# Head of a fused attention and feed-forward kernel: the second slot's first Q and K by shifted weight columns, its first score row earlier, four V tiles moved forward

## The chip, the cores and the metric

The kernel runs as one program on one core of a Trainium2 chip. A core has five engines with a queue of instructions each: TensorE (PE in the profile; its weight loads are PEld) multiplies matrices into the eight banks of PSUM, VectorE (DVE), ScalarE (ACT) and GpSimd (POOL) work elementwise or reduce, and SyncE (SP) issues transfers. Each engine runs its own instructions in the order written and waits at semaphores for the others. The metric is the device time of one execution in microseconds (us), here as the median of several runs.

## The reference

A block with two halves over a sequence of 2048 tokens of 512 features (bfloat16), with 32 heads of 16:

```python
qkv = (layernorm(x) @ wqkv).reshape(B, S, 3, H, Dh) -> q, k, v
scores = einsum("bhqd,bhkd->bhqk", q, k) * (Dh ** -0.5)
p = softmax(scores, axis=-1)
h = x + einsum("bhqk,bhkd->bhqd", p, v).reshape(B, S, D) @ wo
h2 = h + (gelu(layernorm(h) @ w_gate) * (layernorm(h) @ w_up)) @ w_down
```

The scores are 32 x 2048 x 2048, so some 134 million of them pass through a maximum and an exponential; the matrix products beside them are small. The feed-forward half is 1792 wide.

## The kernel before

The 32 heads lie in 8 *slots* of 4 heads. A slot's Q and K are stored transposed, with 16 features of a head at the head of each of four 32-partition groups and room for the negated maximum behind them (`QT`, `KT`). A projection of 128 weight columns yields 8 heads at 16 partitions each: the even heads lie on partitions 0, 32, 64, 96 and are slot `2*ht`; the odd heads lie 16 partitions lower down and are slot `2*ht+1`. To bring those to the right partitions the kernel before copies the projection to `QKS`, moves it up by 16 partitions with a transfer to `QKS2`, and masks the result into `QT` or `KT` on POOL (`item_projT`, and for the first chunk `head_qks` and `head_shift`).

The queries come in 12 *groups* (four of 256 tokens, eight of 128). A group and a slot make a *unit*, 96 in all. Attention runs in two passes over each unit:

- Pass 1 finds the maximum of each query. One *row* is 128 queries of two heads against 512 keys (a *chunk*, `kc`): two matmuls into a pair of PSUM banks (L776) and one DVE reduction over 1024 columns (L779). There are 1024 rows. Unit 0 is the first group and slot 0, unit 1 the first group and slot 1. When a unit's last row is done, POOL joins the maxima, splits them into three bfloat16 parts, a transposing transfer (`STG`) turns them, and POOL adds them to `QT`. Rows 0 to 7 belong to units 0 and 1 and chunk 0; units 8 and 9 (the second group) may lend up to eight rows when the next row isn't ready.
- Pass 2 computes the scores transposed (L927), with the maximum already subtracted through the extra rows, and ACT takes the exponential of 512 columns at a time (L936). There are 2048 of these. They are multiplied by V (L958), and then come normalization, output projection, layernorm, and the feed-forward half of the group, all interleaved with later units.

Nothing of this order is fixed by hand beyond the head: a planner (`Plan`) walks through the program with estimated durations for each instruction and decides what each engine is given next. The estimates (`ivl`, `lat`) therefore shape the order of the whole program, but each engine then simply runs that order and waits where it must. POOL's work comes from a list of jobs with priorities (`jobs.add`, a smaller number first); ACT's statistics come from `act_jobs`; projections and V tiles are *items* that the planner slips in between rows.

The head of the kernel, which the change rewrites, is written out by hand: four tiles of x are normalized and transposed (`head_T`), Q of tokens 0 to 255 and K of tokens 0 to 511 are projected for slot 0 (`head_mm`, then `head_q` and two evacuations), Q of tokens 256 to 511 follows, the four PSUM results are copied once more into `QKS`, and two transfers on SP (L1425) with two masks on POOL (L1430) make slot 1's K and Q. Meanwhile DVE has taken the statistics of x tiles 4 and 5, and ACT takes those of tiles 6 to 15 (`late_stats`, L1466): a sum and a sum of squares per tile. `ln_chain` then finishes them on POOL and normalizes tile by tile (L545), PE transposes each tile (L552), ACT evacuates it to `xnT` (L554), and `item_projT` projects K of the next chunk. V tiles (`item_projV`, matmuls at L714, evacuated by ACT at L590) may start only while few ACT jobs are waiting (`len(act_jobs) <= AJ`).

Of the kernel before, what the change touches and what calls it, by code (L numbers as in the profile page):

```python
# [262 lines left out]
def bass_sequential_preLN__mha_block__geglu_ffn__prompt_kernel(nc, A_x, A_wqkv, A_wo, B_x, B_w_gate, B_w_up, B_w_down, out):  # L263
    with ExitStack() as es:
# [103 lines left out]
        def dve(fn, reads, writes, ivl, lat, extra=()):  # L368
            return P.op("dve", fn, reads, writes, ivl, lat, extra=extra)
# [146 lines left out]

        def ln_norm_act(t):
            act(lambda e: e.activation(out=xn_sb[:, t, :], in_=x_sb[:, t, :], func=ACT.Identity, bias=nmr1[:, t:t + 1], scale=rstd[:, t:t + 1]),
                [("x", t), ("rstd", t), ("nmr1", t)], [("xn", t)], 512, lat=0.79, ivl=0.69)

# [3 lines left out]

        DNORM = {}

        def ln_chain(ts, have_mv):
# [7 lines left out]
            else:  # L535
# [4 lines left out]
            ops += [o(lambda e: e.tensor_tensor(out=rstd[:, sl], in0=rstd[:, sl], in1=nhalf[:, sl], op=ALU.pow), k("rstd") + ["nhalf"], k("rstd"), 0.5 + 0.155 * len(ts), 0.44 + 0.155 * len(ts)),  # L540
                    o(lambda e: e.tensor_tensor(out=nmr1[:, sl], in0=htmp[:, sl], in1=rstd[:, sl], op=ALU.mult), k("rstd") + lk + nk * (not have_mv), nk)]
            for t in ts:
                if t in DNORM:
                    continue
                ops.append(o(lambda e, t=t: e.tensor_scalar(out=xn_sb[:, t, :], in0=x_sb[:, t, :], scalar1=rstd[:, t:t + 1], scalar2=nmr1[:, t:t + 1], op0=ALU.mult, op1=ALU.add),  # L545
                             [("x", t), ("rstd", t)] + nk, [("xn", t)], 0.74, 0.78))
            jobs.add(1, ops)

# [35 lines left out]
        p2_on = [False]  # L584

        def evac(o_ap, i_ap, reads, writes, n, extra=()):
            if p1_over[0] and P.eng["dve"].free <= P.eng["act"].free:
                return dve(lambda e: e.tensor_copy(out=o_ap, in_=i_ap), reads, writes, n / 960.0 + 0.063, n / 960.0 + 0.17, extra=extra)
            last_extra[0] = exps[0]
            return act(lambda e: e.activation(out=o_ap, in_=i_ap, func=ACT.Copy), reads, writes, n, extra=extra)  # L590
# [61 lines left out]
        def item_projT(it, which, ht, c):  # L652
            nm = "w" + which + ("0" if ht == 0 else "")
            tk = list(range(4 * c, 4 * c + 4))
            for d in range(4):
                yield 0.22, [nm] + [("xnT", t) for t in tk], "f"
                b = it.b
                if d == 0:
                    si, s2 = qk_n[0] % 4, qk_n[0] % 2
                    qk_n[0] += 1  # L660
                    qks_busy[("a", si)] = qks_busy[("b", s2)] = True
                for dc in (d,):
                    P.mm(lambda e, dc=dc: e.matmul(pbank[:, b, :], w_cols(which, dc, ht), xnT[:, dc, 512 * c:512 * c + 512], start=(dc == 0), stop=(dc == 3)),
                         reads=[nm] + [("xnT", t) for t in tk], writes=[("pb", b)], n=512, sig=(dc == 3))

# [57 lines left out]

        p1_on = [False]
        seq = []
        steps_of = lambda ui: [(kc, qh, gp) for kc in range(4) for qh in range(nq_of(units[ui][0])) for gp in range(2)]
# [676 lines left out]

        def head_mm(which, b, c0, c1):
            nm = "w" + which + "0"
            xk = [("xnT", t) for t in range(c0 // 128, c1 // 128)]
            for dc in range(4):
                if dc == 0:
                    fill(P.ready("pe", [nm] + xk), 7)
                P.mm(lambda e, dc=dc: e.matmul(pbank[:, b, 0:c1 - c0], w_cols(which, dc, 0), xnT[:, dc, c0:c1], start=(dc == 0), stop=(dc == 3)),  # L1410
                     reads=[nm] + xk, writes=[("pb", b)], n=c1 - c0, sig=(dc == 3))

        def head_q(b, c0, c1, eng):
            keys = [("qT", 0, t) for t in range(c0 // 128, c1 // 128)]
            if eng == "dve":
                return dve(lambda e: e.tensor_scalar(out=QT[:, 0, 0, c0:c1], in0=pbank[:, b, 0:c1 - c0], scalar1=qmask[:, 0:1], scalar2=None, op0=ALU.mult), [("pb", b), "qmask"], keys, 0.33, 0.43)
            else:
                act(lambda e: e.activation(out=QT[:, 0, 0, c0:c1], in_=pbank[:, b, 0:c1 - c0], func=ACT.Copy, scale=qmask[:, 0:1]), [("pb", b), "qmask"], keys, c1 - c0, lat=0.5, ivl=0.4)

        def head_qks(si, b, c0, c1, extra=()):  # L1420
            keys = [("QKSp", si, c0)] + ([("QKS", si)] if c1 == 512 else [])
            return act(lambda e: e.activation(out=QKS[:, si, c0:c1], in_=pbank[:, b, 0:c1 - c0], func=ACT.Copy), [("pb", b)], keys, c1 - c0, extra=extra)

        def head_shift(si, c0, o_ap, keys, s1, s2_):
            P.dma("sp", lambda e: e.dma_start(out=QKS2[0:112, si, :], in_=QKS[16:128, si, :]), ("qks", si), reads=[("QKS", si), ("QKSp", si, 0), ("QKSp", si, c0)], writes=[("QKS2", si)], lat=2.2)  # L1425

            def over(t):
                qks_busy[("a", si)] = qks_busy[("b", si)] = False
                qkv_check()
            jobs.add(1, [(lambda e: e.tensor_scalar(out=o_ap, in0=QKS2[:, si, :], scalar1=s1[:, 0:1], scalar2=s2_[:, 0:1], op0=ALU.mult, op1=ALU.add),  # L1430
                          [("QKS2", si), "qmask", "kmask", "kbias", "zero1"], keys, 0.74, 0.78, ())], then=over)

        for k_ in range(2):
            qks_busy[("a", k_)] = qks_busy[("b", k_)] = True
        qk_n[0] = 2
        qkv_left[0] = 16 + 16 + 16 - 2
        head_T(0)
        head_T(1)
        head_T(2)
        head_mm("q", 6, 0, 256)  # L1440
        t_q = head_q(6, 0, 256, "dve")
        ln_stats(5)
        head_T(3)
        head_mm("k", 4, 0, 384)
        act(lambda e: e.activation(out=KT[:, 0, 0:384], in_=pbank[:, 4, 0:384], func=ACT.Identity, bias=kbias[:, 0:1], scale=kmask[:, 0:1]), [("pb", 4), "kmask", "kbias"], [("kTh", 0)], 384, lat=0.65, ivl=0.55)
        head_mm("k", 5, 384, 512)
        t_k = dve(lambda e: e.tensor_scalar(out=KT[:, 0, 384:512], in0=pbank[:, 5, 0:128], scalar1=kmask[:, 0:1], scalar2=kbias[:, 0:1], op0=ALU.mult, op1=ALU.add), [("pb", 5), "kmask", "kbias", ("kTh", 0)], [("kT", 0, 0)], 0.2, 0.3)
# [9 lines left out]
        DST, AJ = {}, 2  # L1457

        def late_stats(ts):
            left = [2 * len(ts)]  # L1460
            for t in ts:
                for (func, dst, key) in ((ACT.Copy, hsum, "hs1"), (ACT.Square, hsq, "hq1")):
                    pi = 2 * (t - 6) + (func == ACT.Square)

                    def go(t=t, func=func, dst=dst, key=key, pi=pi):
                        act(lambda e: e.activation(out=PTM[:, pi, :], in_=x_sb[:, t, :], func=func, accum_out=dst[:, t:t + 1]), [("x", t)], [(key, t), ("PT", pi)], 512, ivl=0.62, lat=0.95)  # L1466
                        left[0] -= 1
                        if left[0] == 0:
                            ln_chain(ts, False)
                    act_job(go, [("x", t)], [("PT", pi)])  # L1470
        row_hooks = {}
        ln_chain([4, 5], True)
        late_stats([6, 7])
        for t, r in DNORM.items():
# [215 lines left out]
```

## Time and profile before

| | us |
|---|---|
| median of 3 runs | 1240.42 |
| lowest, highest | 1239.35, 1242.41 |
| the profiled execution: its time | 1239.89 |
| the profiled execution: its span | 1238.2 |
| DVE busy | 1191.8 |
| ACT busy | 1195.8 |
| PE busy | 1162.9 |
| POOL busy | 806.1 |
| first row's reduction on DVE starts | 11.93 |
| first exponential on ACT starts | 58.48 |
| last row's reduction on DVE ends | 1199.0 |

The times of the table's last three lines are counted from the start of the span. Most of the program is steady: DVE reduces one row after another, ACT takes one exponential after another, and PE feeds both. What differs from that is the first 60 us, in which rows run but exponentials can't yet, and the last 40 us, in which no rows are left. A busy time counts an instruction from its start to its end, and neighbours overlap a little, so a share near 100% can still hold small gaps.

### The profile page before, as it was taken

To read this page: it belongs to the slowest core of one execution; us is meant where nothing else is said; L and a number is where in the kernel's file an instruction comes from. 1 tells how busy PE (TensorE), PEld (TensorE's weight loads), DVE (VectorE), ACT (ScalarE), POOL (GpSimd) and SP (SyncE) were. 2 spreads that over 40 slices of the span, in tenths; PEclk is the share of its full clock that TensorE was granted. 3 is DMA by queue.
4 is the path that set the end of the run, shared out by engine and by line. 5 is a ranking of instruction groups with operands and counts; after the bars stand their busy time and mean duration, and the time that the engine had idled before them with its cause. 6 is when DMAs were issued, how large, how long until landed. Compare 5 with 4: busy or idle time off the path is not lost.

```text
span 1238.2 us, 39549 instructions
## 1 busy us (share of the span) xinstructions
PE 1162.9 (94%) x16813; PEld 609.8 (49%) x16944; DVE 1191.8 (96%) x1141; ACT 1195.8 (97%) x2515; POOL 806.1 (65%) x1637
## 2 busy tenths in 40 slices
PE   7999999999999999999999999999999999999998
PEld 3333333344333443334345665565666656656666
DVE  6999999999999999999999999999999999999982
ACT  6699999999999999999999999999999999999995
POOL 6757733788537884678727788277584948474854
PEclk8999999999999999999999999999999999999999
DMA  4011150000010000100001000000000010000000
GB/s 145 28 35 35 34 183 21 14 6 4 10 27 13 6 6 12 27 10 3 7 24 18 15 10 10 15 19 6 20 9 19 11 19 10 18 11 10 16 18 11
DMA packets 53137, 28.25 MB, mean 23 GB/s; under 512 B 38240, under 2 KB 51936, under 8 KB 52960
## 3 DMA queue, kind: packets, MB, share of 16 engines
q1 hardware_dynamic: 51904, 25.45, 7.9%
q8 instruction: 133, 2.18, 0.7%
q14 instruction: 44, 0.36, 0.1%
q10 hardware_dynamic: 1056, 0.26, 0.1%
HBM read 11.80 MB, written 2.10 MB: 11 GB/s over the span
## 4 chain that ended last, share of the span: by engine, by line
ACT 55%; DVE 18%; PE 17%; POOL 6%; DMA 2%; issue 2%; SPq 0%; POOLq 0%; DVEq 0%; ACTq 0%
ACT PTM L936 33%; DVE PM L779 17%; ACT PTG L936 9%; ACT PTE L936 5%; PE pbank L927 4%; PE pbank L776 3%; PE pbank L453 2%; PE pbank L1181 2%; ACT g_sb L590 2%; ACT th_sb L1162 2%; PE pbank L1209 2%; PE pbank L958 1%; ACT u_sb L590 1%; POOL LINV L992 1%; ACT OA L590 1%
## 5 line engine op out<-in xcount | busy, mean ns | idle before, releaser
L779 DVE TENSOR_REDUCE PM<-pbank 128x2 f32<-128x1024 f32 x1016 | 1163.8, 1214 | 13.1 <-PE pbank L776 5.3
L936 ACT ACTIVATE PTM<-pbank 128x512 bf16<-128x512 f32 x1388 | 729.1, 656 | 4.3 <-PE pbank L927 2.7
L927 PE MATMUL pbank<-QT,KT 32*128 32x128 bf16 (+1 forms) x6144 | 616.5, 235 | 25.2 <-ACT PTM L936 3.1
L776 PE MATMUL pbank<-KT,QT 32*128 32x512 bf16 x2048 | 400.5, 387 | 24.3 <-DVE PM L779 11.2
L927 PEld LDWEIGHTS pbank<-QT,KT 32*128 32x128 bf16 x6144 | 308.1, 92 | 220.5 <-issue 73.4
L936 ACT ACTIVATE PTG<-pbank 128x512 bf16<-128x512 f32 x420 | 228.2, 661 | 2.0 <-PE pbank L927 0.8
L776 PEld LDWEIGHTS pbank<-KT,QT 32*128 32x128 bf16 x2048 | 97.2, 91 | 181.1 <-DVE PM L779 81.0
L453 PE MATMUL pbank<-ones_bf 128*128 128x512 bf16 (+1 forms) x444 | 134.0, 372 | 9.3 <-issue 1.7
L958 PE MATMUL pbank<-PTM,VA 128*17 128x128 bf16 (+1 forms) x4164 | 133.4, 238 | 1.7 <-ACT PTG L936 0.3
L936 ACT ACTIVATE PTE<-pbank 128x512 bf16<-128x512 f32 x240 | 132.7, 673 | 0.1
L992 POOL TENSOR_TENSOR LINV<-OAT,negone 128x4 f32<-128x4 f32 (+1 forms) x94 | 115.0, 1234 | 19.8 <-ACT OAT L590 19.5
L958 PEld LDWEIGHTS pbank<-PTM,VA 128*17 128x17 bf16 x4164 | 77.2, 90 | 36.5 <-issue 16.5
L860 POOL TENSOR_TENSOR QT<-QT,STG 128x128 bf16<-128x128 bf16 (+1 forms) x95 | 48.3, 508 | 70.0 <-DMA STG<-ST 69.3
L832 POOL CAST ST<-NEGM 128x4 bf16<-128x4 f32 (+1 forms) x95 | 19.7, 208 | 85.5 <-DVE NEGM L840 83.1
L453 PEld LDWEIGHTS pbank<-ones_bf 128*128 128x128 bf16 x524 | 39.6, 98 | 69.9 <-ACT PTM L936 21.7
L815 POOL TENSOR_TENSOR MX<-PM,MX 128x8 f32<-128x8 f32 x94 | 19.0, 202 | 76.7 <-DVE PM L779 73.7
L1168 POOL TENSOR_TENSOR th_sb<-th_sb,g_sb 128x512 f32<-128x512 f32 (+1 forms) x56 | 67.3, 1201 | 1.4
L1164 POOL TENSOR_TENSOR th_sb<-th_sb,g_sb 128x512 f32<-128x512 f32 (+1 forms) x56 | 67.3, 1201 | 1.3
L1152 POOL TENSOR_TENSOR GUT<-th_sb,u_sb 128x512 bf16<-128x512 f32 (+1 forms) x56 | 67.1, 1201 | 1.3
L1181 PE MATMUL pbank<-hnT_l,wu_sb 128*128 128x128 bf16 (+1 forms) x616 | 66.9, 240 | 0.8
L1181 PE MATMUL pbank<-hnT_l,wg_sb 128*128 128x128 bf16 (+1 forms) x616 | 66.2, 242 | 1.2 <-issue 0.3
L1166 POOL TENSOR_TENSOR th_sb<-g_sb 128x512 f32<-128x512 f32 (+1 forms) x56 | 55.3, 988 | 15.3 <-ACT g_sb L590 15.1
(159 smaller groups left out, 1137.6 us busy)
## 6 DMA issues: line engine op xcount, KB each, us to landing
QKS<-QKS SPq DMA_DIRECT2D x32, 112.0 KB, 2.2
xres<-in_A_x_dram SPq DMA_DIRECT2D x16, 128.0 KB, 2.3
out_dram<-out_sb SPq DMA_DIRECT2D x15, 128.0 KB, 1.7
wg_sb<-in_B_w_gate_dram SPq DMA_DIRECT2D x4, 448.0 KB, 5.3
wu_sb<-in_B_w_up_dram SPq DMA_DIRECT2D x4, 448.0 KB, 8.1
x_sb<-in_A_x_dram SPq DMA_DIRECT2D x3, 512.0 KB, 6.6
STG<-ST SPq DMA_TRANSPOSE x96, 2.3
wd_sb<-in_B_w_down_dram SPq DMA_DIRECT2D x3, 512.0 KB, 4.9
```

The source lines that it names most:

```text
L453: P.mm(lambda e: e.matmul(pbank[:, b, 0:n], ones_bf[:, 0:128], ones_bf[:, 0:n], start=True, stop=True), reads=["ones_bf"], writes=[("pb", ...
L776: P.mm(lambda e, g=g, b=b0 + jj: e.matmul(pbank[:, b, :], QT[32 * g:32 * g + 32, c, slot, col:col + 128], KT[32 * g:32 * g + 32, slot, 512 ...
L779: dve(lambda e: e.tensor_reduce(out=pmv(par, kc)[:, qh, 2 * gp:2 * gp + 2], in_=pbank[:, b0:b0 + 2, :], axis=AX.X, op=ALU.max), [("pb", b0 ...
L927: P.mm(lambda e, kt=kt, i=i: e.matmul(pbank[:, b, w * i:w * i + w], KT[32 * g:32 * g + 32, slot, 128 * kt:128 * kt + 128], QT[32 * g:32 * ...
L936: act(lambda e: e.activation(out=PTt(pi), in_=pbank[:, b, :], func=ACT.Exp), [("pb", b)], [("PT", pi)], 512, lat=0.605, ivl=0.48, extra=dX)
L958: P.mm(lambda e, g=g, kt=kt, pi=pi, i=i: e.matmul(pbank[32 * g:32 * g + 17, b, 0:w], VA[:, kt, head(slot, g), :], PTt(pi)[:, w * i:w * i + ...
L992: inv = [((lambda e, a=a: e.tensor_tensor(out=LINV[:, par, a:a + hh], in0=oat[:, a:a + hh, 16], in1=negone[:, 0:hh], op=ALU.pow)), [("OAT" ...
L1152: jobs.add(3, [o(lambda e: e.tensor_tensor(out=o_ap, in0=shp(ts_), in1=shp(us), op=ALU.mult), [kt, ku], [("GUT", fc) for fc in fcs], 1.25, ...
L1164: o(lambda e: e.tensor_tensor(out=ts_, in0=ts_, in1=gs, op=ALU.mult), [kt, kg], [kt], 1.25)], then=second)
L1166: jobs.add(3, [o(lambda e: e.tensor_tensor(out=ts_, in0=gs, in1=gs, op=ALU.mult), [kg], [kt], 1.03, dE), o(lambda e: e.tensor_scalar(out=t ...
L1168: o(lambda e: e.tensor_tensor(out=ts_, in0=ts_, in1=gs, op=ALU.mult), [kt, kg], [kt], 1.25)], then=first)
L1181: P.mm(lambda e, dc=dc, fc=fc, i=i: e.matmul(pbank[:, it.b, w * i:w * i + w], wsb[:, dc, 128 * fc:128 * fc + 128], hT[:, dc, 0:w], start=( ...
```

## The change

Slot 1's first chunk of Q and K is no longer moved by transfers. The two small weight loads of the head bring 144 columns in place of 128, and the same projection is run a second time with the weight columns shifted by 16 (`w_cols(..., sh=16)`), so that the odd heads come out on the even heads' partitions. ACT evacuates the results straight to `KT` and `QT` with scale and bias. The four copies to `QKS`, the two transfers and the two POOL masks of the head go. The first row is issued behind K of slot 1 and ahead of Q of slot 1 and the second half of slot 0's Q. The statistics of tiles 6 and 7 are issued in the head, between its evacuations, and `ln_chain` splits into statistics at priority 0.5 and normalizations at priority 1. V tiles 0 to 3 no longer wait until few ACT jobs are queued (`VE = 4`).

```diff
-        load_w(0, "wq0", 4.0, 0, 128, "act")
-        load_w(1, "wk0", 4.3, 0, 128, "act")
+        load_w(0, "wq0", 4.0, 0, 144, "act")
+        load_w(1, "wk0", 4.3, 0, 144, "act")
...
-        load_w(1, "wk", 7.9, 128, D)
-        load_w(0, "wq", 8.7, 128, D)
+        load_w(1, "wk", 7.9, 144, D)
+        load_w(0, "wq", 8.7, 144, D)
...
-        DNORM = {}
+        DNORM, ANORM = {}, ()
...
-            jobs.add(1, ops)
+
+            def over(tt):
+                for i_, t in enumerate([t for t in ts if t in ANORM]):
+                    act_jobs.insert(i_, (lambda t=t: ln_norm_act(t, nk), [("x", t), ("rstd", t)] + nk, [("xn", t)]))
+                if norms:
+                    jobs.add(1, norms)
+            jobs.add(0.5, ops, then=over)
...
-        def w_cols(which, dc, ht):
-            base = (0 if which == "q" else D) + 128 * ht
+        def w_cols(which, dc, ht, sh=0):
+            base = (0 if which == "q" else D) + 128 * ht + sh
             return wqkv_sb[:, dc, base:base + 128]
...
+        LAG0, LAGX = 2000, lambda n: 60
+
         def evac(o_ap, i_ap, reads, writes, n, extra=()):
-            if p1_over[0] and P.eng["dve"].free <= P.eng["act"].free:
+            if (p1_over[0] and P.eng["dve"].free <= P.eng["act"].free) or (p1_i[0] >= LAG0 and not p1_over[0] and 2 * p1_i[0] - exps[0] > LAGX(p1_i[0])):
...
-            nm = "w" + which + ("0" if ht == 0 else "")
+            nm = ["w" + which + "0"] + ["w" + which] * (ht > 0)
...
+        ops67 = deque()
+        late_stats([6, 7], ops67)
...
+        def head_k(slot, b, c0, c1, key, reads=()):
+            act(lambda e: e.activation(out=KT[:, slot, c0:c1], in_=pbank[:, b, 0:c1 - c0], func=ACT.Identity, bias=kbias[:, 0:1], scale=kmask[:, 0:1]), [("pb", b), "kmask", "kbias"], [key], c1 - c0, lat=(c1 - c0) / 1200 + 0.33, ivl=(c1 - c0) / 1200 + 0.23)
...
         head_mm("k", 4, 0, 384)
-        act(lambda e: e.activation(out=KT[:, 0, 0:384], in_=pbank[:, 4, 0:384], func=ACT.Identity, bias=kbias[:, 0:1], scale=kmask[:, 0:1]), [("pb", 4), "kmask", "kbias"], [("kTh", 0)], 384, lat=0.65, ivl=0.55)
+        head_k(0, 4, 0, 384, ("kTh", 0))
+        ops67.popleft()()
         head_mm("k", 5, 384, 512)
...
-        head_mm("q", 7, 256, 512)
-        head_qks(0, 6, 0, 256, [t_q])
-        head_qks(1, 4, 0, 384)
-        tok = head_qks(1, 5, 384, 512, [t_k])
-        sp_when(P.at[tok], lambda: head_shift(1, 384, KT[:, 1, 0:512], [("kT", 1, 0)], kmask, kbias))
-        tok = head_qks(0, 7, 256, 512)
-        sp_when(P.at[tok], lambda: head_shift(0, 256, QT[:, 0, 1, :], [("qT", 1, t) for t in range(4)], qmask, zero1))
-        head_q(7, 256, 512, "act")
-
+        head_mm("k", 6, 0, 512, 16)
+        head_k(1, 6, 0, 512, ("kT", 1, 0))
+        ops67.popleft()()
+        fill(p1_ready(), 7)
+        p1_issue()
+        head_mm("q", 4, 0, 512, 16)
+        head_q(1, 4, 0, 512, "act")
+        head_mm("q", 5, 256, 512)
+        ops67.popleft()()
+        ops67.popleft()()
+        head_q(0, 5, 256, 512, "act")
         DST, AJ = {}, 2
+        VE = 4
...
-            add_item(*it, can=can_projT if it[0] is item_projT else lambda i_: len(act_jobs) <= AJ)
+            add_item(*it, can=can_projT if it[0] is item_projT else lambda i_: len(act_jobs) <= AJ or i_.args[0] < VE)
```

Line numbers of the changed file are about 10 higher than those of the file before: L776, L779, L927, L936, L590 and L714 there are L786, L789, L937, L946, L599 and L723.

More of the change, by code (lines that the diff above doesn't have):

```diff
@@ L1402, in head_T @@
             ln_T(4 + t % 2, t)
[L1404 to L1431, printed above, removed]
@@ L1453, in bass_sequential_preLN__mha_block__geglu_ffn__prompt_kernel, with late_stats @@
[L1453 to L1459 removed]
+        def late_stats(ts, now=None):
             left = [2 * len(ts)]
@@ L1469, in go, with head_mm @@
                             ln_chain(ts, False)
-                    act_job(go, [("x", t)], [("PT", pi)])
-        row_hooks = {}
+                    if now is None:
+                        act_job(go, [("x", t)], [("PT", pi)])
+                    else:
+                        now.append(go)
+        ops67 = deque()
+        late_stats([6, 7], ops67)
+        def head_mm(which, b, c0, c1, sh=0):
+            nm = "w" + which + "0"
+            xk = [("xnT", t) for t in range(c0 // 128, c1 // 128)]
+            for dc in range(4):
+                if dc == 0:
+                    fill(P.ready("pe", [nm] + xk), 7)
+                P.mm(lambda e, dc=dc: e.matmul(pbank[:, b, 0:c1 - c0], w_cols(which, dc, 0, sh), xnT[:, dc, c0:c1], start=(dc == 0), stop=(dc == 3)),
+                     reads=[nm] + xk, writes=[("pb", b)], n=c1 - c0, sig=(dc == 3))
```

47 lines of the change are left out of this document (26 added, 21 removed).

## The prediction

> **What bounds the kernel now.** I read the busy times first, then the two ends of the program engine by engine, then the waits of the head.
>
> ```profile
> PE 1162.9 (94%) x16813; PEld 609.8 (49%) x16944; DVE 1191.8 (96%) x1141; ACT 1195.8 (97%) x2515; POOL 806.1 (65%) x1637
> ```
>
> DVE and ACT are both nearly full. A stretch of 33 rows on DVE takes 37.41 us in the chain, 1.134 us a row; exponentials follow each other every 0.49 us (21 in 10.59 us, less the overlap). From 11.93 us (first row) to 1199.0 us (last) DVE has 1187 us for 1024 x 1.134 = 1161 us of rows, so it lost some 26 us, and the head is where they lie thickest. DVE's order of time from the head's last evacuation on:
>
> ```profile
> 11.03 0.41 DVE L1447 TENSOR_SCALAR KT<-pbank,kmask,kbias 128x128 bf16<-128x128 f32 x1
> 11.93 4.62 DVE L779 TENSOR_REDUCE PM<-pbank 128x2 f32<-128x1024 f32 x4 [0.49 <-PE pbank L776]
> 19.50 2.35 DVE L779 TENSOR_REDUCE PM<-pbank 128x2 f32<-128x1024 f32 x2 [2.96 <-PE pbank L776]
> 22.30 1.23 DVE L779 TENSOR_REDUCE PM<-pbank 128x2 f32<-128x1024 f32 x1 [0.45 <-PE pbank L776]
> 24.24 1.23 DVE L779 TENSOR_REDUCE PM<-pbank 128x2 f32<-128x1024 f32 x1 [0.71 <-PE pbank L776]
> 26.31 1.22 DVE L779 TENSOR_REDUCE stats<-pbank 128x2 f32<-128x1024 f32 x1 [0.85 <-PE pbank L776]
> ...
> 35.75 24.74 DVE L779 TENSOR_REDUCE PM<-pbank 128x2 f32<-128x1024 f32 x21
> ```
>
> Rows 0 to 15 take 35.75 - 11.93 = 23.82 us in place of 18.14: 5.68 us idle. What ended it, by the waits from 10 to 60 us:
>
> ```profile
> ACT xnT L554 <- PE pbank L552: 6.7, 6, 5.0
> DVE PM L779 <- PE pbank L776: 4.6, 4, 3.0
> PE pbank L776 <- POOL QT L1430: 3.3, 1, 3.3
> POOL KT L1430 <- DMA QKS<-QKS: 3.0, 1, 3.0
> ```
>
> The cause is the fourth line: slot 1's K and Q come by transfers that start at 11.78 us and need 5.32 us in the chain, behind the input loads (their DMA share is 1.10 until 14 us). POOL runs in order, so tiles 6 and 7, whose sums ACT had at 14.2, are normalized only at 21.51; ACT waits 5.0 us for their transposes. PE stands still too, from 15.6 to 18.82 us, and comes back slow:
>
> ```profile
> 16.00:18.00 2.00, 0.00 (x0) 0.00 (x0) 0.54 (x1) 2.00 (x8) 0.82 (x2) 1.00 0.06 18
> 18.00:20.00 2.00, 1.15 (x6) 0.33 (x6) 0.50 (x1) 1.97 (x8) 1.82 (x5) 0.62 0.03 8
> 20.00:22.00 2.00, 1.67 (x7) 0.42 (x7) 1.86 (x2) 0.00 (x0) 1.65 (x5) 0.50 0.00 0
> 22.00:24.00 2.00, 2.00 (x7) 0.39 (x5) 1.23 (x1) 0.00 (x0) 2.00 (x5) 0.50 0.00 0
> ```
>
> (Stretch, length, busy PE, PEld, DVE, ACT, POOL, granted clock, DMA share, GB/s.) At clock 0.50 a row's two matmuls take 0.61 us, not 0.39. At the other end ACT is what counts: it runs without a gap from the last row to 1219.7 us, 37 exponentials and some evacuations, and 18.9 us of serial work follow.
>
> **The change part by part.**
>
> *Removed:* four copies on ACT (1.21 us together), two transfers, two POOL masks (0.77 + 0.78) and POOL's wait of 3.02. *Added:* 8 matmuls of 512 columns on PE (0.216 each, 1.73 in all) and two ACT evacuations (0.68 and 0.50), which about cancel the copies. K of slot 1 stands on PE from about 10.5 to 11.4, before the first row, which waits for DVE's KT at 11.44 anyway: nothing. Row 0 so starts at 11.93 as before.
>
> *Row 1.* Before, rows 0 and 1 are issued together. Now Q of slot 1 (0.86), the other half of slot 0's Q (0.44) and two matmuls of V tile 0 (0.43) stand between them: 11.85 + 1.73 = 13.6, plus 0.44 from issue to reduction (11.49 to 11.93), so row 1 starts at 14.05 while row 0 ends at 13.06: a new gap of 1.0. V's weights are issued to load at 4.23 and that group lands in 8.5, at 12.7; PE reaches them at 13.15. Ends: 0.6 (row 1's wait on V alone, if PE is ahead) to 2.0 (a landing 1 us later); I take 1.0.
>
> *Rows 2 to 15.* K and Q of slot 1 are evacuated by 12.2 and 13.4, and rows 4 to 7 need them at about 17. POOL, free of the wait, runs tiles 6 and 7 from about 14.9: 2.1 of statistics as before, normalization at 17.0 to 18.6, where it was 21.51. PE waits for them ahead of row 6 until 18.6, costing DVE about 0.2. K of chunk 1 is evacuated by 22.2 (before: 29.0), when row 9 needs it. Rows 13 to 16 need slot 1's K of chunk 1 by 27.2; its transfer, on an empty queue, takes 2.2 and POOL's mask ends near 25.7. I add 0.4 for small waits at rows 19 to 27. DVE gains 5.68 - 1.0 - 0.2 - 0.4 = 4.1. Ends: 2.5 (gaps of 0.45 to 0.85, as at rows 6 to 8 before, recur twice) and 5.1 (none).
>
> *Chunks 2 and 3.* These gain less. ACT must finish the sums of tiles 8 to 11 (8 jobs at 0.61, now interleaved with V's evacuations, 0.49 each) and POOL is then held by the joining of unit 0's maxima until row 12 ends, so tiles 8 to 11 are normalized from 29.2, against 29.9. Working on, tiles 12 to 15 come from 37.2 (38.27) and K of chunk 3 at 42.8 (44.91). Unit 0's last four rows start about 43.9 in place of 46.1, so the first exponential comes 2.2 earlier, or up to 3.4 if POOL isn't held by a mask as it was at 51.2. I take 2.6: 55.9.
>
> *V tiles.* Before, 6 of the 16 V evacuations stand behind the first exponential, such as these:
>
> ```profile
> 58.48 1.57 ACT L936 ACTIVATE PTM<-pbank 128x512 bf16<-128x512 f32 x3 [0.51 <-PE pbank L927]
> 59.93 0.62 ACT L590 ACTIVATE VA<-pbank 128x512 bf16<-128x512 f32 x1
> 60.41 0.63 ACT L936 ACTIVATE PTM<-pbank 128x512 bf16<-128x512 f32 x1
> 60.89 0.64 ACT L590 ACTIVATE VA<-pbank 128x512 bf16<-128x512 f32 x1
> ```
>
> In the changed order all 16 stand ahead of it, where ACT has idle time (5.2 us waiting for V's matmuls alone). That takes 6 x 0.49 = 2.9 off ACT's full stretch. Ends: 0 (ACT merely waits longer for rows) and 2.9.
>
> *No cost:* the ACT statistics of tiles 6 and 7 moved into the head (4 x 0.61) delay only slot 0's second Q half, first needed by row 8. SP loses two issues. The new evacuation branch needs row 2000 and there are 1024. The 144-column loads end long before PE's 8.67; 32 KB more at some 300 GB/s is 0.1, at most once.
>
> [...]
>
> *PE's clock.* PE's longest stand in the new head is about 1.1 (before tile 6), against the 3.2 that preceded clock 0.50. Should it fall again, rows would come 1.9 to 2.1 apart as at 22.30 to 26.31, some 0.9 each over four rows: 0 to 3.6; I take 0. [...]
>
> **The sum.** By DVE: rows end 4.1 earlier, and the program order leaves ACT 36 exponentials behind the last row (before 37), two tanh and three evacuations fewer (0.49 + 1.0 + 1.44 = 2.9): 7.0. By ACT: 2.6 + 2.9 = 5.5. Both must finish, so the smaller counts: 1239.9 - 5.5 = 1234.4, made against the profiled execution's own 1239.89 (span 1238.2 and 1.7 around it), which is 0.5 below the median.
>
> **The rivals.**
>
> 1. *DVE's account holds* (exponentials catch up): 1239.9 - 7.0 = 1232.9, down to 1230.5 if row 1's gap is small. For it: the order from row 44 on runs rows and exponentials in step as before. Against: ACT starts only 2.6 earlier.
> 2. *V's evacuations were hidden.* Where ACT waits for rows, their 2.9 become idle time: 2.6 to 4.1 gained, 1235.8 to 1237.3. For it: in either order the exponentials issued stay 33 to 38 behind twice the rows issued from row 700 on, where they were 76 behind at row 60, a sign that ACT has caught up and rows lead there. Against: ACT's unbroken end.
> 3. *The transfers were hidden.* Chunk 3 gates the first exponential and its new V work holds it at 58: about 1239.4. For it: tiles 8 to 11 gain only 0.7.
> 4. *Slower: the thinner lag.* The planner redoes the whole order, and at rows 900, 950 and 1000 exponentials are now 33, 35 and 35 behind, not 34, 36 and 37: 0.5 to 1 us less cover for the maxima's transposes (2.3 median, 4.4 longest). If the 40 units from row 700 on each lose 0.25 more, 10 us go: 1244.4. It decides from 0.24 each (9.7 in all). Against: PE's waits at L927 now end on ACT, 3.1 us in 10.
>
> **How the numbers follow.** Forecast 0.46, rival 1 0.16, rival 2 0.17, rival 3 0.11, rival 4 0.10. A measurement of this kernel tells about 0.3% (3.7 us) from no change, so faster ends at 1236.7 and slower begins at 1244.1. Faster: 0.46 + 0.16 + half of rival 2 = 0.70; same: the other half and rival 3 = 0.20; slower 0.10. The range 1230.5 to 1239.5 leaves out rival 4 and stray ends; the forecast's own is 1232 to 1236.7.
>
> **What would show it.** Right: no transfer to QKS2 before 22 us; one DVE gap near 1.0 behind row 0 and none over 0.5 until 36; granted clock 1.0 from 18 to 26; chunk 3's K near 42.8; first exponential near 55.9 with no V evacuation behind it; last row ending near 1195, last exponential near 1213.8. Wrong: PE standing at V's first matmul; clock 0.50 in the head; the first exponential at 58; or DVE and ACT losing more than before between 200 and 1180.

## The result and the profile after

The changed kernel is slower: 1245.97 us in the median of 22 runs (1239.96 to 1254.01) against 1241.66 in 22 runs of the kernel before. The ratio is 1.0030, 95% interval 1.0017 to 1.0042. Its profiled execution took 1247.2 us with a span of 1245.5, 7.3 us above the span of before. So the forecast of 1234.4 missed by 11.6 us and had the wrong sign, and the range (up to 1239.5) did not hold the time.

The head came out as forecast. DVE's order of time after the change (start, duration, engine, line; L789 is what L779 was):

```profile
10.86 0.41 DVE L1463 TENSOR_SCALAR KT<-pbank,kmask,kbias 128x128 bf16<-128x128 f32 x1
11.76 1.23 DVE L789 TENSOR_REDUCE PM<-pbank 128x2 f32<-128x1024 f32 x1 [0.49 <-PE pbank L786]
13.92 8.01 DVE L789 TENSOR_REDUCE PM<-pbank 128x2 f32<-128x1024 f32 x7 [0.94 <-PE pbank L786]
21.84 1.22 DVE L789 TENSOR_REDUCE stats<-pbank 128x2 f32<-128x1024 f32 x1
22.98 9.30 DVE L789 TENSOR_REDUCE PM<-pbank 128x2 f32<-128x1024 f32 x8
```

One gap of 0.94 us stands behind row 0, and then rows follow without a gap. The stretches of 2 us that stood at clock 0.62 and 0.50 show 1.00 now (stretch and length; PE, PEld, DVE, ACT, POOL busy; granted clock; DMA share, GB/s):

```profile
18.00:20.00 2.00, 2.00 (x17) 0.86 (x15) 2.00 (x3) 1.95 (x5) 1.80 (x4) 1.00 0.04 8
20.00:22.00 2.00, 2.00 (x11) 0.61 (x10) 2.00 (x3) 1.98 (x7) 0.00 (x0) 1.00 0.00 0
22.00:24.00 2.00, 1.79 (x13) 0.84 (x12) 2.00 (x2) 2.00 (x7) 0.00 (x0) 1.00 0.06 19
```

The first exponential follows all of V's evacuations:

```profile
54.38 0.60 ACT L599 ACTIVATE VA<-pbank 128x512 bf16<-128x512 f32 x1 [0.69 <-PE pbank L723]
55.67 0.60 ACT L706 ACTIVATE QKS<-pbank 128x512 bf16<-128x512 f32 x1 [0.69 <-PE pbank L672]
56.52 2.56 ACT L946 ACTIVATE PTM<-pbank 128x512 bf16<-128x512 f32 x5 [0.25 <-PE pbank L786]
```

Row 16 starts at 31.06 us, 4.7 earlier than the 35.75 of before, and this lead was still 6.0 at row 450. It is lost later. From the start of row 16 to the end of the last row the kernel before took 1163.2 us, the changed one 1174.4: 11.2 more. Four spells of half clock (stretches at granted clock 0.50) hold most of it, three of them in rows 800 to 1023:

```profile
538.90:545.70 6.80, 6.80 (x44) 2.87 (x42) 5.45 (x5) 5.66 (x12) 3.91 (x8) 0.50 0.00 1
979.20:986.00 6.80, 6.80 (x114) 4.25 (x114) 4.96 (x6) 4.86 (x11) 5.68 (x11) 0.50 0.01 2
1020.10:1026.90 6.80, 6.80 (x106) 4.43 (x105) 4.58 (x5) 4.88 (x13) 5.40 (x13) 0.50 0.03 7
1194.20:1204.40 10.20, 10.20 (x150) 7.52 (x150) 7.47 (x9) 7.36 (x16) 6.88 (x12) 0.50 0.02 5
sum 30.60, PE 30.60 PEld 19.07 DVE 22.46 ACT 22.76 POOL 21.87; mean PE 7.65 PEld 4.77 DVE 5.62 ACT 5.69 POOL 5.47
```

In these 30.6 us PE is busy throughout, at a granted clock of 0.50 (a row's two matmuls take 0.61 us there, 0.39 elsewhere), and DVE (22.5) and ACT (22.8) stand 8 us each. In the 3.4 us (the shortest spell of the two traces) ahead of the four spells PE was busy for 61, 93, 79 and 88% of the time. The kernel before had three such spells behind its head, 10.2 us in all, with PE busy for 88 to 90% of the 3.4 us ahead:

```profile
206.20:209.60 3.40, 2.92 (x21) 0.86 (x19) 3.26 (x4) 3.05 (x7) 3.10 (x2) 0.50 0.00 0
243.70:247.10 3.40, 3.40 (x19) 0.78 (x17) 3.38 (x4) 2.54 (x6) 3.31 (x4) 0.51 0.19 39
728.40:731.80 3.40, 3.40 (x58) 2.20 (x58) 2.23 (x2) 2.36 (x6) 2.52 (x4) 0.51 0.01 1
sum 10.20, PE 9.72 PEld 3.84 DVE 8.87 ACT 7.94 POOL 8.93; mean PE 3.24 PEld 1.28 DVE 2.96 ACT 2.65 POOL 2.98
```

The row reductions show the same as a group: the idle time ahead of them, and what ended it. First before, then after.

```profile
L779 DVE TENSOR_REDUCE PM<-pbank 128x2 f32<-128x1024 f32 x1016 | 1163.8, 1214 | 13.1 <-PE pbank L776 5.3
```

```profile
L789 DVE TENSOR_REDUCE PM<-pbank 128x2 f32<-128x1024 f32 x1016 | 1165.1, 1216 | 19.0 <-PE pbank L937 12.6
```

Ahead of the exponentials it is the same: ACT's waits from 56 us on for pass 2's matmuls, before and after.

```profile
ACT PTM L936 <- PE pbank L927: 2.7, 6, 0.8
```

```profile
ACT PTM L946 <- PE pbank L937: 9.2, 16, 0.9
```

Each interruption of ACT costs more than its wait: an exponential that follows another takes 0.49 us of its own, one behind a gap 0.60. The changed execution has 70 gaps ahead of exponentials, the one before 44, so 26 x 0.11 = 2.8 us. ACT's account from the first exponential to the end then reads: first exponential 2.0 earlier; no V evacuations behind it, 3.0 less; idle 7.7 more; gaps 2.8 more; and the end 1.5 longer. It gives 7.0 of the 7.3.

The 1.5 of the end is an order of PE. In the last stretch of ACT the copy of the last PV result waits 2.02 us behind the last exponential; before, DVE made that copy 0.48 us behind it. First before, whose last exponential ended at 1219.34, then after:

```profile
1219.82 0.29 DVE L588 COPY OA<-pbank 128x128 f32<-128x128 f32 x1 [4.46 <-PE pbank L958]
```

```profile
1221.12 4.01 ACT L946 ACTIVATE PTM<-pbank 128x512 bf16<-128x512 f32 x8
1227.15 0.28 ACT L599 ACTIVATE OA<-pbank 128x128 f32<-128x128 f32 x1 [2.02 <-PE pbank L968]
```

PE's order there shows why: 14 down projections stand ahead of the last PV matmuls.

```profile
1222.26 1.90 PE L1219 MATMUL pbank<-wd_sb,GUT 128*128 128x512 bf16 x8
1224.09 0.39 PE L937 MATMUL pbank<-QT,KT 32*128 32x128 bf16 x4
1224.41 1.47 PE L1219 MATMUL pbank<-wd_sb,GUT 128*128 128x512 bf16 x6
1225.72 0.38 PE L1223 MATMUL pbank<-xres,ident 128*128 128x512 bf16 x1
```

### The profile page after: what moved, and what is told of

Same layout as the page of the kernel before. It is cut to its first block, busy times and chain, and to the rows that moved or that the text cites. A ratio compares the mean times of both kernels' runs of the same rounds, so it can differ in the third digit from the quotient of the medians.

```text
span 1245.5 us, 39637 instructions
## 1 busy us (share of the span) xinstructions
PE 1196.5 (96%) x16928; PEld 614.2 (49%) x16928; DVE 1195.6 (96%) x1142; ACT 1199.2 (96%) x2512; POOL 801.8 (64%) x1635
## 4 chain that ended last, share of the span: by engine, by line
ACT 43%; DVE 26%; PE 19%; POOL 9%; issue 2%; DMA 1%; POOLq 0%; SPq 0%; DVEq 0%; ACTq 0%
ACT PTM L946 25%; DVE PM L789 25%; ACT PTG L946 7%; PE pbank L937 5%; ACT PTE L946 4%; PE pbank L786 3%; PE pbank L1191 2%; PE pbank L1219 2%; PE pbank L968 2%; POOL LINV L1002 2%; PE pbank L453 2%; ACT th_sb L1172 1%; ACT u_sb L599 1%; ACT g_sb L599 1%; POOL th_sb L1178 1%
## 5 line engine op out<-in xcount | busy, mean ns | idle before, releaser
L789 DVE TENSOR_REDUCE PM<-pbank 128x2 f32<-128x1024 f32 x1016 | 1165.1, 1216 | 19.0 <-PE pbank L937 12.6
L946 ACT ACTIVATE PTM<-pbank 128x512 bf16<-128x512 f32 x1388 | 730.1, 660 | 11.8 <-PE pbank L937 9.2
L937 PE MATMUL pbank<-QT,KT 32*128 32x128 bf16 (+1 forms) x6144 | 615.9, 237 | 19.6 <-ACT PTG L946 1.4
L786 PE MATMUL pbank<-KT,QT 32*128 32x512 bf16 x2048 | 401.3, 388 | 14.3 <-DVE PM L789 8.7
L937 PEld LDWEIGHTS pbank<-QT,KT 32*128 32x128 bf16 x6144 | 307.8, 93 | 212.4 <-issue 69.6
L946 ACT ACTIVATE PTG<-pbank 128x512 bf16<-128x512 f32 x420 | 228.3, 665 | 1.8 <-PE pbank L937 1.3
L786 PEld LDWEIGHTS pbank<-KT,QT 32*128 32x128 bf16 x2048 | 97.3, 91 | 193.3 <-DVE PM L789 93.7
L453 PE MATMUL pbank<-ones_bf 128*128 128x512 bf16 (+1 forms) x500 | 152.5, 375 | 3.4 <-POOL ones_bf L489 1.4
L968 PE MATMUL pbank<-PTM,VA 128*17 128x128 bf16 (+1 forms) x4164 | 135.9, 241 | 1.3 <-ACT PTM L946 0.2
L946 ACT ACTIVATE PTE<-pbank 128x512 bf16<-128x512 f32 x240 | 133.0, 662 | 1.1 <-PE pbank L937 0.8
L968 PEld LDWEIGHTS pbank<-PTM,VA 128*17 128x17 bf16 x4164 | 79.8, 91 | 34.5 <-issue 14.3
L1191 PE MATMUL pbank<-hnT_l,wg_sb 128*128 128x128 bf16 (+1 forms) x616 | 70.0, 245 | 2.1 <-DMA hnT_l<-OnT 1.2
L453 PEld LDWEIGHTS pbank<-ones_bf 128*128 128x128 bf16 x500 | 37.9, 98 | 63.4 <-ACT PTM L946 20.7
L1219 PE MATMUL pbank<-wd_sb,GUT 128*128 128x512 bf16 (+1 forms) x238 | 66.7, 371 | 0.3
```

What stands on the lines that cost most here:

```text
L453: P.mm(lambda e: e.matmul(pbank[:, b, 0:n], ones_bf[:, 0:128], ones_bf[:, 0:n], start=True, stop=True), reads=["ones_bf"], writes=[("pb", ...
L786: P.mm(lambda e, g=g, b=b0 + jj: e.matmul(pbank[:, b, :], QT[32 * g:32 * g + 32, c, slot, col:col + 128], KT[32 * g:32 * g + 32, slot, 512 ...
L789: dve(lambda e: e.tensor_reduce(out=pmv(par, kc)[:, qh, 2 * gp:2 * gp + 2], in_=pbank[:, b0:b0 + 2, :], axis=AX.X, op=ALU.max), [("pb", b0 ...
L937: P.mm(lambda e, kt=kt, i=i: e.matmul(pbank[:, b, w * i:w * i + w], KT[32 * g:32 * g + 32, slot, 128 * kt:128 * kt + 128], QT[32 * g:32 * ...
L946: act(lambda e: e.activation(out=PTt(pi), in_=pbank[:, b, :], func=ACT.Exp), [("pb", b)], [("PT", pi)], 512, lat=0.605, ivl=0.48, extra=dX)
L968: P.mm(lambda e, g=g, kt=kt, pi=pi, i=i: e.matmul(pbank[32 * g:32 * g + 17, b, 0:w], VA[:, kt, head(slot, g), :], PTt(pi)[:, w * i:w * i + ...
```

## The experiments

The theories. **Theory 1:** the head's gain is real, but PE spends more time at half clock behind it. **Theory 2:** the planner redoes the whole order behind any edit, and each redone order has a time of its own, apart from the clock too. **Theory 3:** the change itself costs, through the early V tiles or the early row. Against all three stands that the changed head is worth nothing. *Time at half clock* below is 2 x (1 - mean granted clock) x span, known for every run.

It tells much of each run. Over the changed kernel's 22 runs it went from 9.9 to 65.1 us, and the time with it (correlation 0.94). Over the runs of all kernels here except the one with thin fillers, each kernel taken about its own mean, each us at half clock goes with 0.30 us of time. It differs from run to run, for the spells do not fall on the same rows each time: two executions of the changed order (the second with the edit that follows) had theirs at 539, 979, 1020 and 1194 us, and at 108, 313, 541 and 1217.

**The same order, a fuller array.** 15 more columns of V as weights of each PV matmul, whose results nothing reads (in the code `h` and `n` are arguments of the lambda around the call; here they stand on a line of their own).

```diff
-  e.matmul(pbank[32 * g:32 * g + 17, b, 0:w], VA[:, kt, head(slot, g), :],
+  n = 17 + 15 * (h < H - 1)   # h = head(slot, g)
+  e.matmul(pbank[32 * g:32 * g + n, b, 0:w], VA[:, kt].rearrange("p h i -> p (h i)")[:, 17 * h:17 * h + n],
```

> The changed kernel with every instruction in its place; only the PV matmuls of line 968 use 32 columns of V as weights in place of 17 (the 15 more are the next head's and land in rows of the bank that nothing reads), so PE's array is fuller at the same length of matmul: 6144 x 128 columns a tile, some 3% of the array's work over the span. Theory 1 (half-clock spells): of the 7.3 us between the two profiled spans, 12 lie at the granted clock's spells of 0.50 at 539, 979, 1020 and 1194 us; a fuller array has fewer of them. By the 22 runs of the changed kernel, whose time goes with the time at half clock as 1238.5 + 0.26 for each us of it, a clock of 0.996 (10 us at half) gives about 1241, and the profile shows spells of 10 us or less in all. Theory 2 (the planner's redone order of rows and exponentials is itself worse, whatever the clock): the order is the same, so 1246 as before, also where the clock is nearer to 1.00.

> The same edit in the kernel before. Its profiled execution had 17.1 us at clock 0.50, of which 6.8 in the head, where PE stands still for 3.2 us and 32 columns change nothing. Theory 1: the three spells of 3.4 us behind the head go, 0.26 x 10 = 2.7 us, so about 1239 from 1241.66; the changed kernel with the same edit is then about level with it or up to 4 us faster, since the head's 4.7 us are no longer spent on spells. Theory 2: 1241 to 1242, and the changed kernel with this edit stays 4 us behind it.

Measured: changed 1244.07 (12 runs, 21 us at half clock in the median, ratio to before 1.0022, 0.9999 to 1.0046), before 1243.97 (30 us, ratio 1.0000, 0.9981 to 1.0019). The time at half clock is 8 us less in the one and 5 to 10 more in the other, and both intervals hold 1: this edit does not move the clock in a direction that can be told, and what theory 1 expected of it failed. What it gave is a second execution of each order. Where neither has a spell, a stretch of 50 rows takes the same time to 0.04 us in 23 cases of 26, and to 0.18 in the other three: rows 900 to 950 took 58.86 and 58.88 us in the changed order, 58.04 and 58.00 in the one before. So the orders can be compared with the spells left out. The lesser of the two times, summed over rows 500 to 1000, is 583.3 us changed, 580.3 before: 3.0 us lost at full clock. Over rows 16 to 150 the changed order loses 1.0 and over 150 to 500 it gains 1.1 (for 450 to 500, where both its executions have a spell, by the kernel with the first row behind, further down, whose stretches around it agree to 0.02).

**The same order, a thinner array.** A filler is a matmul whose result nothing reads; it keeps PE busy. Here each filler uses 72 rows and 72 columns of the array.

```diff
-  e.matmul(pbank[:, b, 0:n], ones_bf[:, 0:128], ones_bf[:, 0:n], ...)
+  e.matmul(pbank[0:72, b, 0:n], ones_bf[0:72, 0:72], ones_bf[0:72, 0:n], ...)
```

> The changed kernel with every instruction in its place; only the 500 filler matmuls of line 453 use 72 rows and 72 columns of the array in place of 128 and 128 (a third of the array, at the same length of 512 columns). Theory 1: with less of the array at work there are more spells at clock 0.50: from the 33 us of the profiled execution to 60 to 150 us, and the time goes up by about 0.26 for each us, to 1255 to 1275. Theory 2, or that the clock follows PE's standing still alone: the fillers stand as long as before, so the clock stays at 0.988 to 0.992 and the time at 1246.

Measured: 1302.9, 1309.2 and 1317.2 us (ratio 1.0539, 1.0494 to 1.0584) with 206, 225 and 255 us at half clock, and 1324.5 us with 280 in the execution that was profiled. The clock's row over 40 slices of that execution's span, and two of its spells:

```profile
PEclk9998957899766999669799998799989998979899
```

```profile
161.70:195.80 34.10, 33.63 (x285) 10.70 (x287) 26.31 (x23) 26.12 (x51) 10.39 (x32) 0.50 0.28 88
376.70:414.20 37.50, 37.50 (x279) 10.58 (x281) 27.59 (x24) 27.41 (x53) 17.62 (x47) 0.50 0.06 13
```

Only the fillers' share of the array was altered. At full clock a filler's matmul takes 0.38 us in either kernel, and 53 of the 55 stretches of ten rows without a spell in either take the same time to 0.04 us, so what was lost lies in the spells. PE was busy for 83 to 100% of the 3.4 us ahead of each of the first 20 spells. So here half clock comes with less of the array at work, and not from PE standing still alone, and half clock is a cause of lost time, at (1309.2 - 1246.0) / (225 - 29) = 0.32 us each. The time went beyond the 1255 to 1275 expected because the spells grew beyond the 60 to 150 us expected.

**One part undone, or alone.**

```diff
-        VE = 4
+        VE = 0                          # changed kernel, V not early
```

> The changed kernel without its early V tiles (VE = 0), with the weight shift and the early first row kept. The planner redoes the order. If the early V tiles make the loss (theory 3: they take fillers' and evacuations' places in the head and thin out what PE has for later), the head's gain of some 4 us shows at the end: about 1237 to 1240, with clock 0.993 or higher. If the loss is in the redone middle, where spells fall by chance (theory 1), the time is anything from 1239 to 1250, and goes with the time at half clock: 1238.5 + 0.26 for each us of it.

```diff
-  len(act_jobs) <= AJ)
+  len(act_jobs) <= AJ or i_.args[0] < 4)   # kernel before, V early alone
```

> The kernel before with the early V tiles alone (tiles 0 to 3 exempt from the limit on queued ACT jobs), the transfers of slot 1's first Q and K kept. By the prediction's own step (six V evacuations fewer behind the first exponential, 0.49 each) it gains up to 2.9 on ACT: 1239. If the early V tiles are what makes the changed kernel slow (theory 3), it is slower than before by 3 to 5: 1245 to 1247. By theories 1 and 2 the order is redone and the time can land anywhere from 1239 to 1247, going with the time at half clock.

```diff
         ops67.popleft()()
-        fill(p1_ready(), 7)             # changed kernel, first row
-        p1_issue()                      # not ahead of slot 1's Q
         head_mm("q", 4, 0, 512, 16)
```

> The changed kernel with its first row issued behind the Q projections of slot 1 and the other half of slot 0's Q, not ahead of them. Row 0 then starts some 1.3 us later (8 matmuls, 0.86 + 0.44) and the gap of 0.94 behind it goes, so that row 1 comes at about the same 13.9: nothing gained or lost at row 16. The order behind is redone. Theory 1 or 2: a time of its own between 1240 and 1250, that goes with its time at half clock; if the early row is what costs, 1242 or less with rows 16 to 500 unchanged.

Measured: without early V 1247.24 (ratio 1.0034, 1.0014 to 1.0055); early V alone 1240.20 (1.0001, 0.9983 to 1.0020); first row behind 1245.68 (1.0030, 1.0011 to 1.0049), with row 0 at 13.28 and row 16 at 31.66, 0.6 later than in the changed kernel. With the first row behind, the order from row 250 on takes the changed kernel's time to 0.04 us wherever neither has a spell, and the loss stays: the early row is not its cause. For the V tiles the two runs say less, since each has an order of its own and, by the runs below, such orders differ by several us: leaving them out did not bring the head's gain to the end, and alone they cost nothing that can be told. They moved fewer evacuations than expected, too: with V early alone 2 of the 16 still stand behind the first exponential (before 6), and without early V 3 do in the changed kernel, so the early tiles account for 3 or 4 of the 6.

**The same work in another order.** One number of the planner is altered, and nothing else: COOL, the warmth below which feed-forward pieces are let in early, or PACE, the pace at which they are let in otherwise. The orders are unchanged up to row 203 at the earliest.

```diff
-        PACE, PACEG, COOL = 0.7, 9, 1.7
+        PACE, PACEG, COOL = 0.7, 9, 1.6
```

> The changed kernel with one number of the planner altered: COOL, the warmth below which feed-forward pieces are let in early, 1.6 in place of 1.7. PE's order is the same up to row 213, behind it rows, exponentials, feed-forward pieces and fillers stand in another order (532 fillers in place of 500). No work is added or taken away except fillers. If the head's gain is real and the redone order behind it loses it (theories 1 and 2), another order gives another time: 1240 to 1245, with fewer us at clock 0.50 than the 28.6 of the changed kernel's median run by theory 1 (some 32 more fillers, so 15 to 25), and at the same clock but with fewer interruptions of ACT by theory 2. If the changed head itself costs the time (theory 3 among them), it stays at 1246.

> The kernel before with the same kind of edit and nothing of the change: COOL 1.65 in place of 1.7. PE's order is the same up to row 203 and redone behind it (501 fillers in place of 524). If a redone order by itself moves the time by several us (theory 2), this kernel is slower than 1241.9 by 1 to 5 us without any change of its work, its loss lying behind row 203 in the trace, partly at full clock. By theory 1 alone it moves only with its time at half clock, 0.33 us for each us (the 29 runs of the kernel before: 1234.1 + 0.33 for each us at half clock). If the order hardly matters, it stays within 1 us of 1241.9.

The changed kernel at 1.6 took 1237.25 us, ratio to before 0.9979 (0.9965 to 0.9992): 8.7 us faster than the changed kernel at 1.7, and 4.1 faster than the kernel before. The head is the same in its trace:

```profile
11.78 1.22 DVE L789 TENSOR_REDUCE PM<-pbank 128x2 f32<-128x1024 f32 x1 [0.49 <-PE pbank L786]
13.94 8.01 DVE L789 TENSOR_REDUCE PM<-pbank 128x2 f32<-128x1024 f32 x7 [0.93 <-PE pbank L786]
21.86 1.22 DVE L789 TENSOR_REDUCE stats<-pbank 128x2 f32<-128x1024 f32 x1
...
1221.19 0.28 ACT L599 ACTIVATE OA<-pbank 128x128 f32<-128x128 f32 x1 [0.48 <-PE pbank L968]
```

The last line is from its end: the 2.02 us are back at 0.48; that end takes 18.8 us from the last exponential again. The kernel before at 1.65 went the other way, to 1247.08 (1.0059, 1.0037 to 1.0082), with no change of its work but its fillers. So each order has a time of its own, as theory 2 says, but a large part of it is time at half clock: 0.30 x (28.6 - 16.0) = 3.8 of the 8.7, and 0.30 x (35 - 22) = 4 of the other 5.4. The pairs that follow ask what the change is worth once the luck of an order is averaged out.

> The kernel before with COOL 1.6, the edit that brought the changed kernel to 1237.25. The order is redone behind row 203 (527 fillers, 524 before). Theory 2 (each redone order has a time of its own, and the head's gain is there under all of them): the pair at 1.6 differs by what the head is worth plus the luck of two orders, so this kernel lies at 1239 to 1246, behind the changed kernel at 1.6. The rival (1.6 is simply the better number for both kernels, and the changed head is worth nothing or costs): it comes below 1237.25, at 1233 to 1237.

> The changed kernel with COOL 1.65, at which the kernel before went to 1247.1. The order is redone behind row 213 (521 fillers in place of 500). Theory 2: a time of its own anywhere in 1237 to 1248, with rows 0 to 200 as in the changed kernel (row 16 at 31.1); over the four values of COOL the changed head is ahead in the mean by its 3 to 4.5 us. The rival, that the changed head costs: behind 1247.1 by 4, at 1251.

> The changed kernel with COOL 1.55, again redone behind row 213, with the same number of fillers as at 1.7 (500). Theory 1 (the number of fillers sets the time at half clock): 25 to 30 us at half clock, as at 1.7, and 1245 to 1247. Theory 2: a time of its own in 1237 to 1248.

> The kernel before with COOL 1.55, the pair to the last one; 542 fillers in place of 524. Theory 1: more fillers, less time at half clock: 15 us, 1239 to 1240. Theory 2: a time of its own in 1240 to 1248, behind the changed kernel's at the same number in the mean over the four pairs, by 3 to 4.5 us.

> The kernel before with COOL 1.75; redone behind row 205, 545 fillers in place of 524. The pairs at 1.55, 1.60, 1.65 and 1.70 gave changed minus before of -3.6, -15.0, -3.2 and +4.3. Theory 2 (redone orders scatter by several us around a gain of the head of 3 to 4.5): this kernel at 1242 to 1252, above 1241.9 as at the other three values. The rival (the change itself is worth nothing and the pair at 1.60 was one bad order): the pair differs by less than 3 in either direction.

> The changed kernel with COOL 1.75; redone behind row 210, 532 fillers in place of 500. Theory 2: 1237 to 1248, and 3 to 4.5 below its pair in the mean over all pairs. The rival: level with its pair.

> The kernel before with another number of the planner altered, the pace at which feed-forward pieces are let in: PACE 0.65 in place of 0.7, COOL 1.7 kept. The order is redone behind row 278 (520 fillers). Theory 2: 1241 to 1248. If 1.7 and 0.7 are numbers that suit this kernel's own order, any other value loses here, and 1241.9 is not beaten.

> The changed kernel with PACE 0.65, redone behind row 274 (506 fillers). Theory 2: 1237 to 1248, below its pair by 3 to 4.5 in the mean over the pairs; for the changed order 0.7 and 1.7 are numbers like any other, so values on both sides of 1246 are expected. The rival: level with its pair or above it, as at 0.7.

> The kernel before with PACE 0.75 in place of 0.7, COOL 1.7 kept; the order is redone only behind row 528 (537 fillers). Theory 2: the six pairs so far differ by -3.6, -15.0, -3.2, +4.3, -7.4 and -7.0; this kernel above 1241.6 again, at 1243 to 1249, as at the five other values tried. The rival: at 1241 to 1242, with the changed kernel level or behind.

> The changed kernel with PACE 0.75; its order is redone only behind row 336, and with two fillers more (502) it is close to the changed kernel's own: 1240 to 1247, and by theory 2 below its pair. The rival: level with its pair or behind it, as at 0.7.

Medians in us, and the median time at half clock in brackets:

| planner | kernel before | changed | changed - before |
|---|---|---|---|
| as given (COOL 1.70, PACE 0.70) | 1241.7 (20 to 25) | 1246.0 (29) | +4.3 |
| COOL 1.55 | 1248.8 (37) | 1245.2 (30) | -3.6 |
| COOL 1.60 | 1252.3 (43) | 1237.3 (16) | -15.0 |
| COOL 1.65 | 1247.1 (35) | 1243.9 (27) | -3.2 |
| COOL 1.75 | 1249.6 (27) | 1242.3 (16) | -7.4 |
| PACE 0.65 | 1249.0 (47) | 1242.0 (22) | -7.0 |
| PACE 0.75 | 1242.6 (25) | 1248.2 (32) | +5.7 |

For the kernel before, the numbers as given are the lowest of the seven (PACE 0.75 can't be told from them: 1.0015, 0.9996 to 1.0035); for the changed kernel five of the six others are lower, one of them by only 0.7 us. The change is ahead in five pairs of seven. The two where it is behind are the pair as given and the one that shares most with it: PACE 0.75 redoes the orders only behind rows 336 (changed) and 528 (before). The mean is -3.7 us with a standard error of 2.7 if the seven count as independent, so they lean to a gain but do not settle it. With 0.30 us taken off for each us at half clock (22 for the kernel before as given), the mean is -1.0 with a standard error of 1.4: most of the lean is time at half clock, of which the old head's own spell of 3.4 to 10.2 us, absent in the new one, is a part.

Both ways of losing time show up apart from each other. Before at COOL 1.75 is 8 us above the kernel before with about the same time at half clock (27 against 25): its order is worse at full clock. Before at PACE 0.65 is 7.7 above with 22.6 us more at half clock (47.4 against 24.8), and 0.30 x 22.6 = 6.8 of that is the clock. The number of fillers sets neither: 500 of them went with 29 and 30 us at half clock, 527 with 43, 532 with 16, 16 and 29. In that theory 1's simple form failed. The worst of these traces shows a spell of 23.9 us in the kernel before at COOL 1.60:

```profile
1172.20:1196.10 23.90, 21.94 (x283) 11.48 (x283) 17.37 (x17) 17.64 (x37) 3.85 (x15) 0.50 0.04 10
```

## Why the prediction was wrong

**Right: the head.** Row 0 at 11.76 (forecast 11.93), gap 0.94 (1.0), tiles 6 and 7 normalized at 16.6 (17.0), K of chunk 1 evacuated by 22.1 (22.2), K of chunk 3 at 43.0 (42.8), first exponential at 56.5 (55.9), none of V's evacuations behind it, clock 1.00 from 18 to 26. The 4.1 on DVE came as 4.7. The forecast's own two terms, 2.6 and 2.9, came as 2.0 and 3.0. The head's gain holds in every trace here: row 16 starts between 33.7 and 37.9 us in the nine with the old head, between 31.0 and 31.6 in the nine with the new one, its fillers and its early row. The first exponential comes between 56.8 and 60.6 in the old, between 56.4 and 57.0 in the new. Part of it is chance: where the old head's spell of half clock lasted 3.4 us, row 16 stood at 34.1 and 34.9, and where it did not come at 33.7, so 4.7 is against a spell of 6.8.

**Right in size, not seen in the time: V.** Six evacuations left ACT's full stretch (3.0 against 2.9). V early alone moved four of them and did not make the kernel before faster beyond its interval (0.9983 to 1.0020), in an order of its own.

**Failed: the sum.** It carried 5.5 us from the head to the end and took rows 16 to 1023 and the tail as they were. That term was left out, not mis-sized: +11.2 us between row 16 and the last row, so that the last row ended at 1205.5 us (forecast near 1195) and the last exponential at 1225.1 (1213.8). Of it 9.2 are DVE's idle time in the trace, 6.6 of that within half-clock spells and 8.5 with 1 us on either side of them, and some 1.9 are rows that begin behind a gap and so cannot overlap (one reduction takes 1.22 us, but in a full stretch rows come 1.13 us apart). The planner's order moved with the head, and a lead of 4 us is no larger than what one order differs from another by: the seven orders of the kernel before spread over 10.6 us, those of the changed kernel over 11.

**Failed: the clock.** "PE's longest stand in the new head is about 1.1 ... I take 0" was true of the head, where PE's longest stand from row 0 to row 16 was 0.2 us, but the term covers the head alone. The trace of before already had three spells (206, 244 and 728 us) with PE some 95% busy over the 100 us around each and 88 to 90% busy in the 3.4 us ahead, so no stand like the 3.2 us in its head came before them; no term of the sum holds them. The spells of the two traces behind the head are 3.4, 6.8 and 10.2 us long, and the thin fillers show that a PE that is hardly ever idle (busy for 83 to 100% of the 3.4 us ahead of each of the first 20 spells) falls to half clock as well.

**Failed: the end.** In the sum by DVE, one exponential, two tanh and three evacuations fewer behind the last row were to bring 2.9. In the trace three evacuations and one tanh fewer stand there, and one exponential more (36, before 35). The last exponential ended 0.7 sooner behind the last row (19.7 us against 20.3), and then 14 down projections ahead of the last PV matmuls gave 1.5 back.

**The rivals.** The fourth had the sign, and "The planner redoes the whole order" as its ground, with a chance of 0.10. Its mechanism is not seen: POOL's waits for the maxima's transposes from 600 to 1190 us came to less after the change (39.7 us in 17 waits, before 48.6 in 23), and PE's matmuls of pass 2 waited for the `QT` that POOL makes of them 0.8 us in all. What would prove the forecast wrong was named rightly: between 200 and 1180 us DVE stood 6.0 us longer than before and ACT 4.2. The third rival, the transfers hidden anyway, held the first exponential at 58 us; it came at 56.5. The first two differ from the forecast in what the rows behind the head make of its lead; with 11.2 us lost there, nothing here decides between them.

On the 144-column loads: the forecast gave them 0.1 us at most, at some 300 GB/s (the trace of before shows 237 to 371 in its stretches of 2 us from 2 to 16 us), and no cost of them is seen: row 0 starts at 11.94 us in the mean of the nine traces with the new head, and at 11.99 in the nine with the old one.

**What is shown and what is not.** Shown: the head's gain in its place; that the same changed head with another order behind it beats the kernel before; that another order, with no work but fillers altered, moves the kernel before by up to 10.6 us, of which 0.30 x (43 - 22) = 6 is the clock; that half clock costs about 0.3 us for each us. In the median the changed kernel's +4.3 splits into 0.30 x (29 - 22) = 2 for the clock, and the rest at equal clock. Argued only: which property of an order brings the spells; the thin fillers show one way to bring them, but ahead of two of the changed kernel's four spells PE also stood for 21 and 39% of the 3.4 us. Left open: the change's mean worth (-3.7, standard error 2.7).

## What to carry to other kernels

Where a planner writes the order, an edit in the head is two edits: the head, and a new draw of everything behind it. Size the second by altering a number of the planner that changes no work, in both kernels, before putting a few us down to the first; numbers that suit the old order need not suit the new one. And where PE runs tiles that fill a part of the array, read the granted clock over the whole span, not only where PE stands still (here, with fillers of 72 x 72, 206 us and more went at half clock).

## What the hardware showed unexpectedly

Filler matmuls on 72 x 72 of the array in place of 128 x 128, at the same length and in the same places, brought the time at half clock from 29 us to 206 and more and the time from 1246 us to 1303 and more. Executions of one program, the order fixed, differed between 10 and 65 us at half clock, which is nearly all of their spread of 14 us. Where the clock is full, 50 rows of one order repeat within 0.04 us in 23 cases of 26, and within 0.18 in the others.
